# A lightweight convolution and a gated MLP on one core: one third of block 0's convolution as two TensorE steps over four shifted copies of x

## The chip, the cores and the metric

The kernel runs on one core of one Trainium2 chip. A time is the device time of one execution in microseconds (us). Three executions of the kernel before took 2196.03, 2195.52 and 2195.48 us; the median is 2195.52. A profile is one further execution, recorded by the hardware; its span runs from its first to its last instruction.

The engines are named as in the profile: PE is the matrix engine (TensorE), PEld its weight loads, DVE the vector engine, ACT the scalar engine, POOL GpSimd, SP the engine that here only issues DMAs. L231 means line 231 of the kernel before.

## The reference

Only the shapes and formulas that matter are kept.

```python
# x: (8, 4096, 192) f32; weight: (8 heads, 7 taps) f32
w = softmax(weight, axis=-1)
y[b, s, c] = sum_k w[head(c), k] * x_pad[b, s + k, c]     # 6 zeros ahead of each sequence
# y as (32768, 192); w_in: (192, 2048); w_out: (2048, 192), both scaled by a float64 number
h = y @ w_in
g = h * clip(h + 3.0, 0.0, 6.0) / 6.0
out = (g @ w_out).astype(float32)
```

Each head owns 24 channels. The two weight matrices arrive as 64-bit floating-point numbers; x and the taps are 32-bit.

## The kernel before

**Tiling.** The 32768 tokens are cut into 32 blocks of 1024, each in two halves of 512. x is laid out with channels first. A channel is 3p + s, with p from 0 to 63 and s from 0 to 2: partitions 0 to 63 of a tile hold the 64 values of p for the first half of the tokens, partitions 64 to 127 the same for the second half, and s, called a third, is an axis of the free dimension. Six columns ahead of the tokens hold the tokens before (zeros at the head of a sequence).

**First layer.** The hidden units are 16 chunks of 128. Every f32 product is made of three passes in a reduced format: high part of the weight by high part of y, low part by high part, full weight by low part of y (`PASSES`). So y of each third is split into high (`high_of`, ACT) and low (`low_of`, DVE: y minus high). A unit n of the first layer is one chunk, for both halves of the tokens: `products` issues, per third, six matmuls, two per pass, one on each half of the partitions. Units 0 to 7 take y as it is (`y_own`); units NP to NP + 7 (NP is 8) take `y_other`, in which the two halves of the partitions are swapped by two DMAs per part and third (`swap`, SP, L304 and L305). With the results in PSUM, ACT makes `relu` (L316) and DVE `gate` (L320) writes the hidden value into g.

**Second layer.** It multiplies g by w_out; in block 0 directly (`direct_chunk`, L331), in later blocks by a recursive scheme with fewer products.

**Rounding of the weights.** A unit of 384 weights per partition comes in by DMA as 64-bit words and becomes f32 in four steps of class `Rounding`: `split` (two integer operations on DVE, L192 and L196), `clamp` (three on ACT, L204, L207, L210), `join` (two on DVE, L213 and L217, then a product on POOL, L221), and for w_in `part`: the high part on ACT (L229), a full copy (L230) and the low part, full minus high (L231), both on POOL. The units are, in order, w_in 0, w_in 1, w_in 2, w_out 0, w_in 3, w_out 1 and so on.

**Block 0.** Its start is written out by hand; each engine runs its instructions in the order of the source (`manual_schedule`, from L909). Third 2 is convolved on PE: seven matmuls with a diagonal matrix per tap (`pe_tap`, L924) into PSUM bank b, after three matmuls of zeros (L932). Third 0 is convolved on DVE, seven taps of two cuts each (`conv_units`, L289 and L293). Third 1 is shared: tap 0 on ACT (L938), tap 1 on DVE, taps 2 to 6 on PE in bank b1, and a DVE addition (L983) puts the parts together. The order around this is:

```python
high_y(pe_third, psum[:, b : b + 1])     # ACT, then two swaps on SP
part(0)                                  # ACT L229, POOL L230 and L231
for u in conv0[per - 3 : per]:           # the last three DVE operations of third 0
    u()
low_y(pe_third, psum[:, b : b + 1])      # DVE L428, then two swaps
high_y(0, all_of(0))                     # ACT L425, then two swaps
low_y(0, all_of(0))
thirds_of(0, pe_third, 0)                # unit 0: thirds 2 and 0
thirds_of(NP, pe_third)                  # unit NP: third 2, from y_other
```

After that come unit w_in 1 (split, clamp, join, part), the end of third 1, the loads for later, `thirds_of(0, 1, end=True)` and `thirds_of(NP, 0)`. A loop over 16 steps (from L1026) then runs units in the order 0, 1, NP, NP + 1, 2, NP + 2 and so on. Each step issues the products of its unit (none for unit 0, the last third for unit NP), the relu, the steps of the weight units that are due, the gate, and from step 5 on every second step 16 products of the second layer.

**Queues.** SP issues, in this order, part of x, w_in 0, third 1 of x (two DMAs), w_in 1, w_in 2, w_out 0, w_in 3; then the swaps as their data come; then further weights and x of block 1. POOL issues third 2 of x, ACT the upper half of third 0.

Of the kernel before, what the change touches and what calls it, by code (L numbers as in the profile page):

```python
# [11 lines left out]
F32 = mybir.dt.float32  # L12
# [19 lines left out]
def kernel(  # L32
# [20 lines left out]
    K3 = D // D2  # L53
# [7 lines left out]
    NP = NC // 2  # L61
    DH = D // 2
    QS = 32
# [30 lines left out]
    for base, dma in ((0, nc.scalar), (D2, nc.sync)):  # L94
        dma.dma_start(
            out=w_sb[base : base + D2],
            in_=weight.unsqueeze(1).to_broadcast([H, GJ, KC]),
# [6 lines left out]
    def load_x0(s, dma_lower, dma_upper):  # L104
        head, lower, upper = x_source(0)
        dma_lower.dma_start(out=x_tiles[0][0:D2, s, head:], in_=lower[:, s])
        dma_upper.dma_start(out=x_tiles[0][D2:P, s, :], in_=upper[:, s])
# [6 lines left out]
    make_identity(nc, ident[:])  # L114
    diag = cnv.tile([P, KC, P], F32, name="diag", bufs=1)
    g = cst.tile([P, NP, 2, G, N], F32, name="g")
    mx = ot.tile([P, 1], F32, name="mx")
    zeros = g[:, 0, 0, 0]
    nc.vector.memset(zeros, 0.0)
# [31 lines left out]
    def load_w_in(j):  # L151
        st = early_stages[j]
        for half in range(2):
            nc.sync.dma_start(
                out=st[half * D2 : (half + 1) * D2].rearrange("p (s f) w -> p s (f w)", s=K3),
                in_=w_in_bits[j + half * NP].rearrange("p s f w -> p s (f w)"),
            )
        return st
# [14 lines left out]
    class Rounding:  # L173
# [4 lines left out]

        def __init__(self, load, dst):
            self.load_words, self.dst = load, dst

        def load(self):
            self.st = self.load_words()
# [1 line left out]
        def split(self, engine=nc.vector):  # L187
            high = self.st[:, :, 1]
            self.top = cnv.tile([P, WS], U32, name="top")
            self.scale = cnv.tile([P, WS], U32, name="scale")  # L190
            self.sig = cnv.tile([P, WS], F32, name="sig")
            engine.tensor_scalar(  # L192
                out=self.scale[:], in0=high, scalar1=0x7FF00000, scalar2=None,
                op0=ALU.bitwise_and,
            )
            engine.tensor_scalar(  # L196
                out=self.top[:], in0=high, scalar1=0xFFFFF, scalar2=0x100000,
                op0=ALU.bitwise_and, op1=ALU.bitwise_or,
            )
# [12 lines left out]
        def join(self):  # L212
            nc.vector.scalar_tensor_tensor(  # L213
                out=self.scale[:], in0=self.st[:, :, 1], scalar=0x80000000,
                in1=self.scale[:], op0=ALU.bitwise_and, op1=ALU.bitwise_or,
            )
            nc.vector.scalar_tensor_tensor(  # L217
                out=self.sig[:], in0=self.top[:], scalar=2.0**-20, in1=self.sig[:],
                op0=ALU.mult, op1=ALU.add,
            )  # L220
            nc.gpsimd.tensor_tensor(  # L221
                out=self.sig[:] if len(self.dst) > 1 else self.dst[0],
                in0=self.sig[:], in1=self.scale[:].bitcast(F32), op=ALU.mult,
            )

        def part(self):
            if len(self.dst) > 1:
                high, low, full = self.dst
                nc.scalar.mul(r32(high), self.sig[:], CUT)  # L229
                nc.gpsimd.tensor_copy(out=r32(full), in_=self.sig[:])  # L230
                nc.gpsimd.tensor_tensor(  # L231
                    out=r32(low), in0=self.sig[:], in1=high, op=ALU.subtract
                )

    def r32(ap):
        return ap.bitcast(F32R)

    def w_in_unit(j):
        dst = [w[:, j].rearrange("p s f -> p (s f)") for w in w_in_parts]
        return Rounding(lambda: load_w_in(j), dst)  # L240

    def w_out_unit(j):
        dst = w_out[:, j, B11 : B22 + 1].rearrange("p b d -> p (b d)")
# [14 lines left out]
    for n in range(5):  # L258
        units[n].load()
        if n == 0:  # L260
            load_x0(1, nc.sync, nc.sync)

    nc.vector.tensor_reduce(out=mx[:], in_=w_sb[:], axis=AX.X, op=ALU.max)
    e_sb = cst.tile([P, KC], F32, name="e_sb")
# [1 line left out]
        out=e_sb[:], in0=w_sb[:], in1=mx[:].to_broadcast([P, KC]), op=ALU.subtract  # L266
# [3 lines left out]
    c_sb = cst.tile([P, KC], F32, name="c_sb")  # L270
# [5 lines left out]
    y = ys.tile([P, K3, N], F32, name="y")  # L276
    OWN, OTHER = range(2)

    def conv_units(i, parts, cuts=1):


        x = x_tiles.pop(i)
        W = N // cuts

        def tap(part, k, t):
            c = c_sb[:, k : k + 1]
            to = y[:, part, t : t + W]
            if k == 0:
                nc.vector.tensor_scalar(  # L289
                    out=to, in0=x[:, part, t : t + W], scalar1=c, scalar2=None, op0=ALU.mult  # L290
                )
            else:
                nc.vector.scalar_tensor_tensor(  # L293
                    out=to, in0=x[:, part, k + t : k + t + W], scalar=c, in1=to,
                    op0=ALU.mult, op1=ALU.add,
                )

        return [
            lambda part=part, k=k, t=t: tap(part, k, t)
            for part in parts for k in range(KC) for t in range(0, N, W)  # L300
        ]

    def swap(to, part):
        nc.sync.dma_start(out=to[D2:P], in_=part[0:D2])  # L304
        nc.sync.dma_start(out=to[0:D2], in_=part[D2:P])  # L305
# [6 lines left out]
    psum = ps.tile([P, 2 * 4, N], F32, name="psum")  # L312
# [96 lines left out]
    def add(out, x, y, op=ALU.add):  # L409
        nc.vector.tensor_tensor(out=out, in0=x, in1=y, op=op)  # L410
# [13 lines left out]
    def high_of(out, x):  # L424
        nc.scalar.mul(r32(out), x, CUT)  # L425

    def low_of(out, x, high, engine):
        engine.tensor_tensor(out=r32(out), in0=x, in1=high, op=ALU.subtract)  # L428
# [480 lines left out]
    with tc.manual_schedule():  # L909
# [4 lines left out]
            out=c_sb[:], in0=e_sb[:], in1=sm[:].to_broadcast([P, KC]), op=ALU.mult  # L914
# [2 lines left out]

        thirds = [slice(s, s + 1) for s in range(K3)]
        pe_third = K3 - 1
        pe_taps = 2  # L920
        x0 = x_tiles[0]

        def pe_tap(b, part, k, first):
            nc.tensor.matmul(  # L924
                out=psum[:, b], lhsT=diag[:, k], rhs=x0[:, part, k : k + N],
                start=(k == first), stop=(k == KC - 1),
            )

        b, b1 = (2 * free_slots[-1] + k for k in range(2))
        for _ in range(3):  # L930

            nc.tensor.matmul(  # L932
                out=psum[:, b], lhsT=zeros[:, 0:P], rhs=zeros, start=True, stop=True
            )
        for k in range(KC):
            nc.scalar.mul(diag[:, k], ident[:], c_sb[:, k : k + 1])
            pe_tap(b, pe_third, k, 0)
        nc.scalar.mul(y[:, 1], x0[:, 1, 0:N], c_sb[:, 0:1])  # L938
        for k in range(pe_taps, KC):
            pe_tap(b1, 1, k, pe_taps)  # L940

        early = {}

        def thirds_of(n, *which, end=False):
            if n not in early:
                early[n] = free_slots.pop(0)
            for s in which:
                products(n, early[n], s, begin=s == pe_third, end=end)

        def high_y(s, of):  # L950
            high_of(y_own[HIGH][:, thirds[s]], of)
            swap(y_other[0][:, HIGH, thirds[s]], y_own[HIGH][:, thirds[s]])

        def low_y(s, of):
            low_of(y_own[LOW][:, thirds[s]], of, y_own[HIGH][:, thirds[s]], nc.vector)
            swap(y_other[0][:, LOW, thirds[s]], y_own[LOW][:, thirds[s]])

        def all_of(s):
            return y[:, thirds[s]]

        conv0 = conv_units(0, thirds[:pe_third], 2)
        per = len(conv0) // pe_third
        for u in conv0[:5]:
            u()
        split(0)
        clamp(0)
        for u in conv0[5 : per - 3]:
            u()
        join(0)
        high_y(pe_third, psum[:, b : b + 1])  # L970
        part(0)
        for u in conv0[per - 3 : per]:
            u()
        low_y(pe_third, psum[:, b : b + 1])
        high_y(0, all_of(0))
        low_y(0, all_of(0))
        thirds_of(0, pe_third, 0)
        thirds_of(NP, pe_third)
        split(1)
        clamp(1)  # L980
        for u in conv0[per + 2 : per + 2 * pe_taps]:
            u()
        add(y[:, 1], psum[:, b1], y[:, 1])  # L983
        high_y(1, all_of(1))
        join(1)
        part(1)
        low_y(1, all_of(1))
        for n in (5, 6, 7, 8):
            load(n)
        x_tiles[1] = load_x(1)  # L990
        split(2)
        clamp(2)
        thirds_of(0, 1, end=True)
        thirds_of(NP, 0)

        def conv_jobs(i, add_last=False):

# [28 lines left out]
        for r in range(2 * NP):  # L1026
            k = order[r]
# [11 lines left out]
            n = joins.get(r)  # L1039
# [128 lines left out]
```

## Time and profile before

| What | Value |
|---|---|
| Median of three executions | 2195.52 us |
| The profiled execution's own time | 2195.4 us |
| Its span | 2193.6 us |
| Granted PE clock over the span | 0.999 |
| First matmul of the first layer (L443) | starts at 17.18 us |
| First relu (L316) | starts at 22.63 us |
| Second relu | starts at 23.83 us |

The page gives, for each engine, the busy time, its share of the span and the number of instructions; the chain that ended last, followed back from the last instruction through what released each step; groups of instructions with the mean duration; and the DMA issues. The timeline gives for each row the start, the duration over all instructions of the row, the engine, the line, the operation, output and inputs, the shape, and how many; in brackets stands the idle time before it and what ended that. A row with the engine's name and a q behind it is the queue that issues, so SPq is SP issuing a DMA. Matmuls of f32 appear twice per call, as two instructions.

### The profile page before, as it was taken

What the parts mean: (1) busy time and instruction counts of PE and PEld (TensorE: products, weight loads), DVE (VectorE), ACT (ScalarE), POOL (GpSimd) and SP (SyncE); (2) the same over time, 40 slices, a digit from 0 to 9 for tenths busy, and PEclk for the clock granted to TensorE, in tenths of its full rate; (3) what the DMA queues carried; (4) which work ended last, traced back from release to release, by engine and by line L of the source; (5) the groups of instructions that cost most, each with busy time, mean ns of one, the idle gap of its engine ahead of it and who ended that gap; (6) DMA issues with size and microseconds to landing.
All of it is one profiled execution on the core that took longest, in us unless ns stands there. A gap on an engine that the chain in (4) does not pass through costs nothing.

```text
span 2193.6 us, 53710 instructions
## 1 busy us (share of the span) xinstructions
PE 2185.0 (100%) x23086; PEld 1564.3 (71%) x23086; DVE 1979.9 (90%) x1871; ACT 1271.8 (58%) x1761; POOL 1018.1 (46%) x867
## 2 busy tenths in 40 slices
PE   9999999999999999999999999999999999999998
PEld 5577777777777777777777777777777777777776
DVE  8889899889899898998989988999999999898987
ACT  7456565565655665555656556565566555565644
POOL 4545543355433555334554335553355543455433
PEclk9999999999999999999999999999999999999999
DMA  7366556756567665666655675656666566765564
GB/s 166 66 120 98 97 99 111 128 90 107 97 111 121 103 109 91 110 112 120 98 97 100 112 127 90 107 98 112 121 106 106 91 110 112 122 97 97 99 105 64
DMA packets 329821, 231.80 MB, mean 106 GB/s; under 512 B 208816, under 2 KB 293296, under 8 KB 329584
## 3 DMA queue, kind: packets, MB, share of 16 engines
q0 software_dynamic: 98752, 122.35, 36.6%
q1 hardware_dynamic: 229320, 105.73, 23.8%
q8 instruction: 181, 2.97, 0.6%
q10 hardware_dynamic: 1512, 0.30, 0.1%
q14 instruction: 56, 0.46, 0.1%
HBM read 31.72 MB, written 25.17 MB: 26 GB/s over the span
## 4 chain that ended last, share of the span: by engine, by line
PE 98%; ACT 1%; DVE 0%; POOL 0%; DMA 0%; issue 0%; POOLq 0%; DVEq 0%
PE psum L583 49%; PE psum L443 47%; PE psum L331 2%; PE psum L924 0%; PE psum L932 0%; ACT g L316 0%; DVE results L410 0%; DMA y_other<-y 0%; POOL w_in L231 0%; ACT scale L207 0%; POOL out_dram L357 0%; ACT sig L204 0%; ACT sig L210 0%; POOL sig L221 0%; DVE xt L833 0%
## 5 line engine op out<-in xcount | busy, mean ns | idle before, releaser
L583 PE MATMUL psum<-g,w_out 128*32 128x512 f32 (+1 forms) x5720 | 1023.8, 508 | 0.0
L316 ACT ACTIVATE g<-psum,half 128x1024 f32<-128x1024 f32 x512 | 571.5, 1116 | 312.4 <-PE psum L443 311.2
L583 PE MATMUL psum<-s,w_out 128*32 128x512 f32 (+1 forms) x3272 | 735.5, 570 | 0.9 <-DVE results L410 0.9
L320 DVE SCALAR_TENSOR_TENSOR g<-g,psum 128x1024 f32<-128x1024 f32 x512 | 609.4, 1212 | 133.1 <-ACT g L316 132.8
L541 POOL TENSOR_TENSOR s<-g 128x256 f32<-128x256 f32 x248 | 254.3, 1025 | 751.3 <-DMA out_dram<-results 538.5
L583 PEld LDWEIGHTS psum<-g,w_out 128*32 128x32 f32 x5720 | 421.4, 110 | 171.1 <-issue 61.6
L443 PE MATMUL psum<-y,w_in 64*128 64x512 f32 x4608 | 534.3, 388 | 0.3
L443 PE MATMUL psum<-y_other,w_in 64*128 64x512 f32 x4608 | 529.0, 386 | 0.0
L443 PEld LDWEIGHTS psum<-y,w_in 64*128 64x128 f32 x4608 | 428.6, 184 | 120.7 <-issue 26.0
L443 PEld LDWEIGHTS psum<-y_other,w_in 64*128 64x128 f32 x4608 | 431.6, 184 | 91.0 <-DMA y_other<-y 0.4
L1007 DVE SCALAR_TENSOR_TENSOR y<-x,c_sb,y 128x1536 f32<-128x1536 f32 x156 | 306.1, 1962 | 1.9 <-ACT y L1004 1.8
L583 PEld LDWEIGHTS psum<-s,w_out 128*32 128x32 f32 x3272 | 227.9, 110 | 106.6 <-issue 54.3
L583 PE MATMUL psum<-g,w_s 128*32 128x256 f32 x1488 | 289.3, 379 | 0.0
L390 POOL TENSOR_TENSOR s<-g 128x1024 f32<-128x1024 f32 x93 | 236.9, 2717 | 0.4 <-DVE g L320 0.4
L583 PE MATMUL psum<-z,w_s 128*32 128x256 f32 x992 | 235.1, 380 | 0.0
L390 DVE TENSOR_TENSOR s<-g 128x1024 f32<-128x1024 f32 x124 | 188.9, 1543 | 1.1
L583 PEld LDWEIGHTS psum<-g,w_s 128*32 128x32 f32 x1488 | 149.8, 110 | 32.0
L583 PE MATMUL psum<-s,w_s 128*32 128x256 f32 x744 | 170.7, 379 | 0.0
L483 ACT ACTIVATE z<-g 128x512 f32<-128x512 f32 x186 | 142.6, 767 | 18.5 <-DVE g L320 18.5
L410 DVE TENSOR_TENSOR g<-g 128x1024 f32<-128x1024 f32 x124 | 143.6, 1220 | 1.1
L410 DVE TENSOR_TENSOR results<-psum,results 32x256 f32<-32x256 f32 (+2 forms) x221 | 107.9, 488 | 39.1 <-PE psum L583 33.8
L541 POOL TENSOR_TENSOR s<-s,g 128x256 f32<-128x256 f32 x124 | 136.4, 1100 | 9.7
(115 smaller groups left out, 2347.8 us busy)
## 6 DMA issues: line engine op xcount, KB each, us to landing
y_other<-y SPq DMA_DIRECT2D x124, 384.0 KB, 5.1
z<-g POOLq DMA_DIRECT2D x93, 512.0 KB, 5.6
z<-z POOLq DMA_DIRECT2D x62, 512.0 KB, 5.4
out_dram<-results SPq DMA_DIRECT2D x375, 64.0 KB, 2.6
y<-x POOLq DMA_DIRECT2D x30, 768.0 KB, 8.9
x<-in_x_dram SPq DMA_DIRECT2D x53, 388.5 KB, 7.4
g<-g POOLq DMA_DIRECT2D x31, 512.0 KB, 6.4
g<-in_moe_w_in_dram SPq DMA_DIRECT2D x16, 192.0 KB, 5.5
```

The source lines that it names most:

```text
L316: nc.scalar.activation(r6, h, ACT.Relu, bias=half[:], scale=1.0 / 6.0)
L320: nc.vector.scalar_tensor_tensor(out=g_, in0=g_, scalar=1.0, in1=h, op0=ALU.min, op1=ALU.mult)
L331: lambda p=p: nc.tensor.matmul(out=bank[j * QS : (j + 1) * QS, tokens], lhsT=w_out[:, p, w, cols], rhs=x[:, p, tokens], start=(first and p ...
L390: engine.tensor_tensor(out=o[:, r], in0=a[:, r], in1=b[:, r], op=op)
L410: nc.vector.tensor_tensor(out=out, in0=x, in1=y, op=op)
L443: nc.tensor.matmul(out=psum[:, 2 * slot + k], lhsT=r32(w_in_parts[wn][r, c, s]), rhs=r32(y_other[0][r, yn, s] if group else y_own[yn][r, s ...
L483: nc.scalar.mul(to, x, sign)
L541: engine.tensor_tensor(out=o, in0=p, in1=q, op=op)
L583: nc.tensor.matmul(out=out, lhsT=w, rhs=x, start=start, stop=True, tile_position=(0, j * QS), skip_group_check=True,)
L1007: nc.vector.scalar_tensor_tensor(out=y[:], in0=taps_of(k), scalar=c_sb[:, k : k + 1], in1=y[:], op0=ALU.mult, op1=ALU.add,)
```

## The change

Third 1 of block 0's convolution is no longer shared by three engines. Four copies of its x are loaded (`x_quads`), each on 32 partitions and each shifted by one more token; both token halves stand in one row of 1028 columns, and the 64 values of p are split into two groups a of 32. A matrix of 128 by 32 (`quad_diag`) holds four taps' diagonals, one below the other, so that one matmul does four taps of 32 channels; step j = 0 does taps 0 to 3, step j = 1 taps 4 to 6. The eight matmuls (two steps, two halves, two groups) write the four 32-partition strips of bank b1. The copies into `quad_diag` are eight small ACT operations. The memory of `x_quads` is the part of g of chunks 2 and 3, which is not in use yet.

Tap 0 on ACT, tap 1 on DVE, five taps on PE and the addition for third 1 go; its high and low parts are taken from bank b1.

Unit w_in 0 becomes urgent: its product and its low part move from POOL to DVE and its full copy from POOL to ACT. The other units stay.

The order changes too: after join(0) come high_y(2), part(0) and then five DVE operations of third 0 (three before, with two fewer ahead of join(0)); split(1) moves ahead of high_y(0); third 0 of unit NP moves ahead of third 1 of unit 0; low_y(1) moves ahead of part(1).

```diff
+    QW = TB + 4
+    x_quads = (
+        g[:, 2:4].rearrange("p c h k n -> p (c h k n)")[:, : 2 * QW]
+        .rearrange("p (a u) -> p a u", a=2)
+    )
+    nc.vector.memset(x_quads[:, :, 0:PAD], 0.0)
+    quad_diag = cnv.tile([P, 2, 2, QS], F32, name="quad_diag", bufs=1)
+    nc.gpsimd.memset(quad_diag[3 * QS :, :, 1], 0.0)
+
+    def load_x_quads(s, dma):
+        rows_ = xT[0].rearrange("(a p s) t -> s p a t", a=2, s=K3)[s]
+        for r in range(4):
+            dma.dma_start(
+                out=x_quads[r * QS : (r + 1) * QS, :, PAD - r :],
+                in_=rows_[..., 0 : QW - PAD + r],
+            )
...
-            nc.gpsimd.tensor_tensor(
+            (nc.vector if self.urgent else nc.gpsimd).tensor_tensor(
                 out=self.sig[:] if len(self.dst) > 1 else self.dst[0],
...
-                nc.gpsimd.tensor_copy(out=r32(full), in_=self.sig[:])
-                nc.gpsimd.tensor_tensor(
+                if self.urgent:
+                    nc.scalar.copy(out=r32(full), in_=self.sig[:])
+                else:
+                    nc.gpsimd.tensor_copy(out=r32(full), in_=self.sig[:])
+                (nc.vector if self.urgent else nc.gpsimd).tensor_tensor(
                     out=r32(low), in0=self.sig[:], in1=high, op=ALU.subtract
...
-            load_x0(1, nc.sync, nc.sync)
+            load_x_quads(1, nc.sync)
...
+        def quad_weights():
+            for r in range(4):
+                for a in range(2):
+                    ch = slice(a * QS, (a + 1) * QS)
+                    ks = range(r, KC, 4)
+                    nc.scalar.copy(
+                        out=quad_diag[r * QS : (r + 1) * QS, a, 0 : len(ks)],
+                        in_=diag[ch, r::4, ch],
+                    )
+
+        def pe_quads(b):
+            for j in range(2):
+                for h in range(2):
+                    for a in range(2):
+                        q = 2 * h + a
+                        nc.tensor.matmul(
+                            out=psum[q * QS : (q + 1) * QS, b], lhsT=quad_diag[:, a, j],
+                            rhs=x_quads[:, a, h * N + 4 * j : (h + 1) * N + 4 * j],
+                            start=j == 0, stop=j == 1,
+                            tile_position=(0, q * QS), skip_group_check=True,
+                        )
...
-        nc.scalar.mul(y[:, 1], x0[:, 1, 0:N], c_sb[:, 0:1])
-        for k in range(pe_taps, KC):
-            pe_tap(b1, 1, k, pe_taps)
...
-        conv0 = conv_units(0, thirds[:pe_third], 2)
-        per = len(conv0) // pe_third
+        conv0 = conv_units(0, thirds[:1], 2)
         for u in conv0[:5]:
             u()
         split(0)
         clamp(0)
-        for u in conv0[5 : per - 3]:
+        quad_weights()
+        pe_quads(b1)
+        for u in conv0[5:9]:
             u()
         join(0)
         high_y(pe_third, psum[:, b : b + 1])
         part(0)
-        for u in conv0[per - 3 : per]:
+        for u in conv0[9:]:
             u()
         low_y(pe_third, psum[:, b : b + 1])
+        split(1)
         high_y(0, all_of(0))
         low_y(0, all_of(0))
         thirds_of(0, pe_third, 0)
-        thirds_of(NP, pe_third)
-        split(1)
+        thirds_of(NP, pe_third, 0)
         clamp(1)
-        for u in conv0[per + 2 : per + 2 * pe_taps]:
-            u()
-        add(y[:, 1], psum[:, b1], y[:, 1])
-        high_y(1, all_of(1))
+        high_y(1, psum[:, b1 : b1 + 1])
         join(1)
+        low_y(1, psum[:, b1 : b1 + 1])
         part(1)
-        low_y(1, all_of(1))
...
         thirds_of(0, 1, end=True)
-        thirds_of(NP, 0)
```

More of the change, by code (lines that the diff above doesn't have):

```diff
@@ L173, with __init__ @@
     class Rounding:
-        def __init__(self, load, dst):
-            self.load_words, self.dst = load, dst
+        def __init__(self, load, dst, urgent=False):
+            self.load_words, self.dst, self.urgent = load, dst, urgent
         def load(self):
@@ L236, in r32 @@
         return ap.bitcast(F32R)
+    URGENT = 1
     def w_in_unit(j):
         dst = [w[:, j].rearrange("p s f -> p (s f)") for w in w_in_parts]
-        return Rounding(lambda: load_w_in(j), dst)
+        return Rounding(lambda: load_w_in(j), dst, j < URGENT)
     def w_out_unit(j):
@@ L919, with pe_tap @@
         pe_third = K3 - 1
-        pe_taps = 2
         x0 = x_tiles[0]
-        def pe_tap(b, part, k, first):
+        def pe_tap(b, part, k):
             nc.tensor.matmul(
                 out=psum[:, b], lhsT=diag[:, k], rhs=x0[:, part, k : k + N],
-                start=(k == first), stop=(k == KC - 1),
+                start=(k == 0), stop=(k == KC - 1),
             )
+        def quad_weights():
[18 more added lines that the diff above has]
+                        )
         b, b1 = (2 * free_slots[-1] + k for k in range(2))
@@ L936 @@
             nc.scalar.mul(diag[:, k], ident[:], c_sb[:, k : k + 1])
-            pe_tap(b, pe_third, k, 0)
-        nc.scalar.mul(y[:, 1], x0[:, 1, 0:N], c_sb[:, 0:1])
-        for k in range(pe_taps, KC):
-            pe_tap(b1, 1, k, pe_taps)
+            pe_tap(b, pe_third, k)
         early = {}
```

## The prediction

> **What bounds the kernel now.** I read the page's busy rows first, then the chain that ended last in order of time over the first 60 us, then each engine's timeline there.
>
> ```profile
> PE 2185.0 (100%) x23086; PEld 1564.3 (71%) x23086; DVE 1979.9 (90%) x1871; ACT 1271.8 (58%) x1761; POOL 1018.1 (46%) x867
> ```
> ```profile
> PE 98%; ACT 1%; DVE 0%; POOL 0%; DMA 0%; issue 0%; POOLq 0%; DVEq 0%
> ```
>
> TensorE (PE) is the bound of the whole; what is not PE on the chain lies in the start. A start that is x us shorter or longer moves the end by about x, as everything behind it is one PE stream. The edit touches only the first 25 us. The chain there (start, us, what):
>
> ```profile
> 6.95 6.02 PE psum L924 x14
> ...
> 13.00 0.60 ACT y L425
> ...
> 22.14 1.67 PE psum L443 x12
> ...
> 23.83 1.12 ACT g L316
> ...
> 35.26 3.71 PE psum L443 x30
> ```
>
> The reader is to see the hand-over at 23.83. From that second relu (unit 1, L316) ACT runs without a gap to 34.1, through relus, clamps and the high part of w_in 3 at 33.59; POOL's subtraction at 34.18 follows, and at 35.26 PE has its operands and never starves again. That 11.4 us relay is untouched by the diff. So the price of the edit is the shift of this relu, which waits for the last matmul of products(1). What sets that today is on the weight-load queue (PEld) and SP:
>
> ```profile
> 18.28 0.59 SPq L305 DMA_DIRECT2D y_other<-y  x1
> ```
> ```profile
> 20.64 0.19 PEld L443 LDWEIGHTS psum<-y_other,w_in 64*128 64x128 f32 x2 [0.40 <-DMA y_other<-y]
> ...
> 22.14 1.22 PEld L443 LDWEIGHTS psum<-y,w_in 64*128 64x128 f32 x12 [0.57 <-POOL w_in L231]
> ```
>
> The swap of low(third 0) is issued at 18.28 and its landing lets PE on at 20.64: 2.35 us. PE then waits for w_in 1's low part at 22.14, runs twelve loads, and the relu starts 0.47 after the last (23.36 to 23.83). SP issues one pair of swaps every 1.28 us (starts at 16.42, 17.70, 18.98, 20.27), whatever its data do.
>
> DVE and ACT in the stretch that is rewritten:
>
> ```profile
> 8.84 2.46 DVE L293 SCALAR_TENSOR_TENSOR y<-x,c_sb,y 128x256 f32<-128x256 f32 x6
> 11.21 0.55 DVE L213 SCALAR_TENSOR_TENSOR scale<-g,scale 128x384 uint32<-128x384 uint32 x1
> 11.73 0.56 DVE L217 SCALAR_TENSOR_TENSOR sig<-top,sig 128x384 f32<-128x384 uint32 x1
> 12.21 2.26 DVE L293 SCALAR_TENSOR_TENSOR y<-x,c_sb,y 128x256 f32<-128x256 f32 x3
> 14.50 0.69 DVE L428 TENSOR_TENSOR y<-psum,y 128x512 fp32r<-128x512 f32 x1
> ```
> ```profile
> 13.00 0.60 ACT L425 ACTIVATE y<-psum 128x512 fp32r<-128x512 f32 x1 [1.29 <-PE psum L924]
> 13.58 0.52 ACT L229 ACTIVATE w_in<-sig 128x384 fp32r<-128x384 f32 x1
> ```
>
> Taps cost 0.41 each while POOL is idle and 0.75 beside POOL's three operations of unit 0 (12.38 to 15.33). ACT reaches the high part of w_in 0 (L229) only after high_y(2), which waits for PE's taps until 13.00.
>
> **The change part by part.**
>
> PE, third 1: five taps go, ten matmuls at a pitch of 0.43 (24 from 6.77 to 17.25), 4.3 us. In come eight 32-column matmuls, sixteen instructions. Nearest row: L331, 128*32 128x512, 32 in 3.64 us, four side by side; sixteen are 1.75. PE would finish at 12.97 + 1.75 = 14.7 instead of 17.25, plus at most the 0.35 and 0.84 that PEld idles on entering L331 and returning to L443. This gain is worth nothing unless PE then has operands.
>
> ACT: tap 0 of third 1 goes (L938, 0.72, which waited for x to 9.24), so clamp(0) starts at about 8.68, when the first split operation is done, and ends at 10.53. Eight small copies for quad_weights follow: between the 0.21 of the 128x7 exponential and the 0.29 pitch of the seven 128x128 diagonals (2.15 us for seven); I take 0.25, nearer the small end: 2.0, over at 12.5 (bounds 12.2 and 12.9). Hidden, since high_y(2) waits for PE to 13.0 anyway. The full copy of w_in 0 comes to ACT: 0.52, to 14.6, before anything else there is ready.
>
> SP and DMA: two loads of x (0.26 MB) become four of 0.26 MB: 0.79 MB and two issues (1.2 us) more, ahead of w_in 1, 2, 3 and w_out 0 on SP. At the 245 GB/s that the slices show at 8 to 9 us that is 3.2 us: the last copy lands at about 9.1 + 3.3 = 12.4 (today's x lands for 9.24), w_in 1 at about 14.3, the queue runs dry near 17.6 instead of 14.3. Cover: PE has nothing to do after the quads until 17.3 (below), and split(1) is reached at 17.3. Priced at nothing; cover gone, each us late is a us.
>
> POOL loses unit 0's 1.17 + 0.58 + 1.15; the two memsets are 0.1 at most in the idle start.
>
> DVE: taps 1 and the add of third 1 go (0.87 + 0.69); unit 0's product and subtraction come (about 0.55 each, as L213). But their place adds a wait. Taps 5 to 8 now end at 10.5, join(0) with its product at 12.0. The next DVE instruction is the subtraction high-from-full of unit 0, which needs ACT's L229: 13.58 + 0.52 = 14.1. DVE, in order, stands from 12.0 to 14.1 with five taps behind it that need nothing. Today POOL did this wait while DVE went on. Then: subtraction to 14.6; five taps at 0.41, to 16.7; low_y(2), 0.69, to 17.36 (today 15.19).
>
> From there everything that feeds PE is late:
> - Swaps: low(2) is issued at 17.39 (today 15.22), high(0) at 18.67, low(0) at 19.95 and, its second half, 20.53. It lands 2.35 later: 22.88 (today 20.63).
> - w_in 1: split(1) 17.3 to 17.9; clamp(1) on ACT 17.67 to 19.5; high_y(1) to 20.15; join(1) to 20.1; POOL's product to 21.2 (1.02; 21.5 at the 1.40 it took today), its low part by 22.85 to 23.2 (today 22.09).
> - PE: thirds_of(NP, 2, 0) now stands ahead of third 1 of unit 0. So when low(0) lands at 22.88, two loads of it, six of third 1 and eighteen of products(1) are still to run: 26 at 0.113 (18 in 2.04, L443) is 2.94, last load over at 25.8, relu at 25.8 + 0.47 = 26.3. The w_in 1 low part is asked for after fourteen of them, at 24.5: covered by 1.3.
>
> Sum: 26.3 against 23.83, **+2.5 us**. The relay behind it keeps its length, as its own ACT work and PE's work after products(1) are the same. On the profiled execution, 2195.4 (span 2193.6, 0.12 under the median 2195.52), that is **2197.9**. Bounds of the terms: copies (none), swap pitch 1.20 to 1.29 (-0.2), landing 2.3 to 2.4, join and taps (+-0.3), memset ahead of the warm-up matmuls (+0.1): 2197.0 to 2198.8 if the mechanism holds.
>
> The clock: the same 128x512 f32 matmul took 1.04 to 1.22 us for the first six (L932) and 0.59 from L924 on, so PE starts at about half pace, though the granted clock reads 1.00 in every slice. [...]
>
> **The rivals.**
>
> 1. No stall, no loss. If DVE could run the five taps before the subtraction (ACT through with L229 by 12.0, or another order on DVE than the source's), low(2) would be issued at 14.9 as the first pair ends, low(0)'s second half at 18.0, land at 20.4, and the relu start at 23.8: no change, 2195.4; with the pair pitch at 1.0 (the shortest issue is 0.46) 0.7 less, 2194.7. It decides if low(0)'s second half is issued before 18.07. Against: ACT idled 1.29 for PE before 13.00, and every DVE operation today stands in source order. The 0.4 us or more needed for a real gain isn't there even so: the swap queue takes over.
>
> [...]
>
> 3. The loads behind the copies come late. w_in 1 has 14.3 to 17.3 at DVE plus the 1.3 at PE in hand; at the 106 GB/s of the 14 to 15 us slice the 1.05 MB would take 9.9 us from 8.1, w_in 1 would land near 21.7, 4.4 after DVE wants it, and the end be 3 later still: 2201. Against: while loads alone run, no slice from 4 to 14 us is under 219.
>
> **How the numbers follow.** The stall case has 0.75, rival 1 0.12, rival 2 0.08, rival 3 0.05. Predicted 2197.9. The range reaches from just under rival 1's no-change end, 2195.2, to 2199.9: it leaves out rivals 2 and 3 and rival 1's lower half, 0.19. 0.2%, about what a measurement of this kernel can tell from no change, is 4.4 us: 2191.1 to 2199.9. No case gives 2191; 0.01 for what I haven't seen. Slower: most of rivals 2 and 3 and a tail of the first, 0.09. Within: 0.90.
>
> **What would show it.** Right: DVE idle about 2.1 us before the subtraction at 14.1, released by ACT's high part; low(2) issued near 17.4; PEld waiting for y_other until near 22.9; sixteen quad matmuls in about 1.75 us; the second L316 relu near 26.3 and PE unbroken from about 37.7. Wrong: taps on DVE between 12 and 14, quads held by x_quads past 16, split(1) waiting for its load, matmuls of 0.2 us pitch near 23, or a relay of another length than 11.4.

## The result, and the profile after

The changed kernel takes 2200.05 us (median; 2198.50 to 2200.64) where the kernel before takes 2195.74 beside it: +4.3 us, a ratio of 1.0019 with a 95% interval of 1.0012 to 1.0027. That is 0.15 above 2199.9, the upper end of the forecast's range around 2197.9. The profiled execution took 2199.41 us with a span of 2197.6, 4.0 more than before. New line numbers are 19 to 25 higher: L231 is now L253, L229 L248, L293 L318, L425 L450, L428 L453, L304 and L305 L329 and L330, L316 L341, L443 L468, L331 L356. New are L958, the copies into `quad_diag`, and L968, the quad matmuls.

TensorE is the bound as before. The row of busy times on the page of the kernel after:

```profile
PE 2185.2 (99%) x23092; PEld 1565.2 (71%) x23092; DVE 1974.9 (90%) x1871; ACT 1272.7 (58%) x1769; POOL 1014.0 (46%) x865
```

PE has the same 2185 us to do, so the loss is idle time and slower work in the start. The chain there, kernel after (start, us, what):

```profile
18.93 3.71 DMA y_other<-y
...
22.69 5.63 PE psum L468 x25
...
28.34 1.12 ACT g L341
...
38.66 1.03 POOL w_in L253
...
39.73 3.71 PE psum L468 x30
```

The second relu starts at 28.34 instead of 23.83, 4.5 later. From it to the unbroken PE stream at 39.73 it is 11.39 us, against 11.43 before: the relay has kept its length, as forecast, and everything happened before 28.34. In place of the short wait for w_in 1 the chain now has a DMA of 3.71 us, a swap, ahead of PE's products.

The forecast's own steps first. The timelines of DVE, then of ACT, kernel after:

```profile
13.87 0.56 DVE L253 TENSOR_TENSOR w_in<-sig,w_in 128x384 fp32r<-128x384 f32 x1 [1.73 <-ACT w_in L248]
14.34 2.06 DVE L318 SCALAR_TENSOR_TENSOR y<-x,c_sb,y 128x256 f32<-128x256 f32 x5
16.43 0.69 DVE L453 TENSOR_TENSOR y<-psum,y 128x512 fp32r<-128x512 f32 x1
```
```profile
10.55 1.97 ACT L958 COPY quad_diag<-diag 32x64 f32<-32x64 f32 x8
...
13.31 0.52 ACT L248 ACTIVATE w_in<-sig 128x384 fp32r<-128x384 f32 x1
```

DVE stands idle for 1.73 us until ACT's high part of w_in 0 is there; the five taps and low_y(2) come behind. So the wait that the forecast was built on is real. The timeline of SP's queue, kernel after:

```profile
17.15 0.46 SPq L329 DMA_DIRECT2D y_other<-y  x1
...
20.23 0.59 SPq L330 DMA_DIRECT2D y_other<-y  x1
```

The first half of low(2)'s swap is issued at 17.15 (forecast 17.39), the second half of low(0)'s at 20.23 (forecast 20.53). Up to the issue of the swaps the forecast holds within 0.3 us. What follows is the timeline of the weight loads, kernel after:

```profile
20.68 0.50 PEld L468 LDWEIGHTS psum<-y_other,w_in 64*128 64x128 f32 x4 [2.17 <-DMA y_other<-y]
...
22.69 0.50 PEld L468 LDWEIGHTS psum<-y_other,w_in 64*128 64x128 f32 x4 [0.72 <-DMA y_other<-y]
23.69 0.29 PEld L468 LDWEIGHTS psum<-y_other,w_in 64*128 64x128 f32 x2 [0.50 <-DMA y_other<-y]
23.85 4.01 PEld L468 LDWEIGHTS psum<-y,w_in 64*128 64x128 f32 x24
```

PE gets low(0) at 23.69, not 22.88: 0.8. And the last 26 loads take from 23.69 to 27.86, 4.17 us, not 2.94: 1.2. Together 2.0, the distance from the forecast 26.3 to 28.34. Two other views of the kernel after name the two causes. The tile view of `y_other` over the first 32 us gives the time from a swap's issue to its landing, first after, then before:

```profile
DMA to landing us min/median/max: 2.8/3.7/6.6
```
```profile
DMA to landing us min/median/max: 2.3/2.3/2.4
```

Each swap took 2.3 us before; now the first one used, high(2), needs 6.6, and the next ones land one pair per 1.0 us: high(2) near 20.6, low(2) 21.7, high(0) 22.6, low(0) 23.7. The windows of 1 us, kernel after (us; busy time and count of PE, PEld, DVE, ACT, POOL; granted PE clock; DMA share; GB/s):

```profile
18.00:19.00 1.00, 0.73 (x4) 0.19 (x2) 0.54 (x2) 0.94 (x3) 0.00 (x0) 1.00 1.13 225
...
20.00:21.00 1.00, 0.32 (x2) 0.32 (x4) 1.00 (x2) 0.02 (x1) 0.94 (x1) 0.50 1.07 262
...
25.00:26.00 1.00, 1.00 (x8) 0.70 (x8) 0.00 (x0) 0.19 (x1) 0.48 (x1) 0.50 0.75 261
...
27.00:28.00 1.00, 1.00 (x12) 0.82 (x10) 1.00 (x1) 0.00 (x0) 0.00 (x0) 1.00 0.91 204
```

The same view of the kernel before:

```profile
14.00:15.00 1.00, 1.00 (x4) 0.43 (x3) 0.97 (x2) 0.60 (x2) 1.00 (x2) 1.00 0.48 106
...
20.00:21.00 1.00, 1.00 (x8) 0.39 (x6) 1.00 (x2) 0.55 (x2) 0.94 (x2) 1.00 0.92 209
```

Before, the loads have ended in the slice from 14 us, where the share drops to 0.48. In the kernel after, the DMA engines stay full until past 20 us (share 1.0 or more in every slice from 4 us on but one, of 0.94), because 0.79 MB more stand ahead of the swaps. And the granted clock falls to 0.50 shortly before 20 (0.90 in the slice from 19, 0.50 in the six from 20), where it was 1.00 before, and comes back in the slice from 26 (0.69): at 25 PE starts 8 matmuls in a microsecond, at 27 twelve.

### The profile page after: what moved, and what is told of

It reads as the page before. It is cut to its first block, busy times and chain, and to the rows that moved or that the text cites. A ratio compares the mean times of both kernels' runs of the same rounds, so it can differ in the third digit from the quotient of the medians.

```text
span 2197.6 us, 53730 instructions
## 1 busy us (share of the span) xinstructions
PE 2185.2 (99%) x23092; PEld 1565.2 (71%) x23092; DVE 1974.9 (90%) x1871; ACT 1272.7 (58%) x1769; POOL 1014.0 (46%) x865
## 4 chain that ended last, share of the span: by engine, by line
PE 98%; ACT 1%; DVE 0%; POOL 0%; DMA 0%; issue 0%; POOLq 0%; SPq 0%; DVEq 0%
PE psum L608 49%; PE psum L468 48%; PE psum L356 2%; PE psum L948 0%; PE psum L978 0%; ACT g L341 0%; DMA y_other<-y 0%; DVE results L435 0%; ACT scale L226 0%; ACT sig L223 0%; DVE y L318 0%; POOL out_dram L382 0%; DVE xt L858 0%; ACT w_in L248 0%; POOL p L821 0%
## 5 line engine op out<-in xcount | busy, mean ns | idle before, releaser
L341 ACT ACTIVATE g<-psum,half 128x1024 f32<-128x1024 f32 x512 | 571.4, 1116 | 317.0 <-PE psum L468 316.8
L468 PE MATMUL psum<-y,w_in 64*128 64x512 f32 x4608 | 535.4, 389 | 1.5 <-DVE y L453 1.3
L468 PE MATMUL psum<-y_other,w_in 64*128 64x512 f32 x4608 | 530.6, 387 | 2.1 <-DMA y_other<-y 2.1
L468 PEld LDWEIGHTS psum<-y,w_in 64*128 64x128 f32 x4608 | 429.7, 184 | 122.5 <-issue 26.8
L468 PEld LDWEIGHTS psum<-y_other,w_in 64*128 64x128 f32 x4608 | 432.1, 184 | 94.3 <-DMA y_other<-y 3.9
```

Source lines behind the costliest of these rows:

```text
L341: nc.scalar.activation(r6, h, ACT.Relu, bias=half[:], scale=1.0 / 6.0)
L468: nc.tensor.matmul(out=psum[:, 2 * slot + k], lhsT=r32(w_in_parts[wn][r, c, s]), rhs=r32(y_other[0][r, yn, s] if group else y_own[yn][r, s ...
```

## The experiments

**The theories.** Theory A is the forecast's: the wait on DVE makes the swaps late. Theory B: the copies' bytes make them late, since the swaps land behind the loads that SP issued earlier. A third part can add to either: the halved clock. All edits are made on the changed kernel unless another is named. Times are medians, beside the kernel before, measured together with each (2195.5 to 2195.7).

The table has, for each run, when PE's weight loads got low(0) and when the second relu started, both in its profile, and the time against before. A halved clock is a granted clock of 0.50 in two or more of the slices of 1 us, a full one is 1.00 in every slice from 15 to 28 us.

| Run | Wait on DVE | Bytes ahead of the swaps | Clock in the profile | low(0) at PE, us | Second relu, us | Against before, us |
|---|---|---|---|---|---|---|
| Kernel before | no | as before | full | 20.64 | 23.83 | 0 |
| Changed kernel | yes | +0.79 MB | halved | 23.69 | 28.34 | +4.3 |
| e1_no_stall | no | +0.79 MB | halved | 23.79 | 28.87 | +4.1 |
| e2_loads_later | yes | loads moved behind | halved, early | 23.35 | 26.63 | +3.8 |
| e3_both | no | loads moved behind | halved | 20.89 | 25.53 | +1.8 |
| e4_warm | yes | +0.79 MB | full | 23.52 | 26.82 | +2.7 |
| e5_both_warm | no | loads moved behind | full | 21.16 | 24.43 | +1.7 |
| e6_order | no | loads moved behind | full | no wait for it | 24.28 | +1.7 |
| e7_before_copies | kernel before | +0.79 MB | full | 23.64 | 26.25 | +2.2 |
| e8_swaps_pool | no | +0.79 MB, later loads too | halved | 26.47 | 31.10 | +7.5 |
| e9_no_stall_warm | no | +0.79 MB | full | 23.64 | 26.95 | +4.0 (+2.6 in the group of the profile) |
| e10_one_copy | yes | as before | full | 22.36 | 25.65 | +2.5 |
| e11_one_copy_no_stall | no | as before | full | 20.65 | 23.96 | +0.5 |
| e12_pairs | no | +0.26 MB | full | 21.15 | 23.75 | -0.4 |

**e1_no_stall: the wait taken away.** The high and low part of w_in 0 come behind the five taps.

```diff
-        part(0)
         for u in conv0[9:]:
             u()
+        part(0)
```

> The five DVE taps of third 0 stand ahead of unit 0's subtraction, nothing else moves, so DVE no longer waits 1.73 us for ACT. Theory A, the forecast's: the wait makes the swaps late. Then low(2) is issued near 15.3 instead of 17.15, the second half of low(0) near 18.3 and lands 2.35 later, at 20.7; the second relu starts near 24.1 and the time is about 2196.0. Theory B: the swaps lie in SP's DMA queue behind 0.79 MB more of loads, the last of which (w_in 3) lands near 19.5, and land one pair per 1.0 us after that, whenever they are issued. Then low(0) still lands at 23.6 and PE is held as now: the second relu at 27 to 28.4, the time 2198.8 to 2200.0.

Measured: 2199.63 (2198.70 to 2200.63), ratio 1.0019 (1.0009 to 1.0029). Nothing is won. low(2) is issued at 15.69, 1.5 earlier than in the changed kernel, yet the timelines of the weight loads and of ACT in this run read:

```profile
20.73 0.44 PEld L468 LDWEIGHTS psum<-y_other,w_in 64*128 64x128 f32 x4 [3.70 <-DMA y_other<-y]
...
23.79 0.29 PEld L468 LDWEIGHTS psum<-y_other,w_in 64*128 64x128 f32 x2 [0.52 <-DMA y_other<-y]
```
```profile
28.87 1.12 ACT L341 ACTIVATE g<-psum,half 128x1024 f32<-128x1024 f32 x1 [1.85 <-PE psum L468]
```

The swaps land at the same times as with the wait, to 0.1 us: issued 1.5 us earlier, low(2) only takes longer to land here. Theory A falls as the only cause.

**e2_loads_later: the queue ahead of the swaps made shorter.** Two of the units that are loaded ahead of the swaps, w_out 0 and w_in 3, come behind them.

```diff
-    for n in range(5):
+    for n in range(3):
...
-        for n in (5, 6, 7, 8):
+        for n in (3, 4, 5, 6, 7, 8):
```

> The loads of w_out 0 and w_in 3 (0.79 MB, as much as the copies add) are issued after the last swap instead of ahead of the first; the DVE wait stays. Theory A: swaps are issued as now (low(2) at 17.15, low(0)'s second half at 20.2); they land 2.35 to 3.5 later; a gain of at most 1.2, if the clock stays halved 2198.8. Theory B: the queue is empty before 17, every swap lands 2.35 after its issue, high(2) near 16.4, so PE works on unit NP from 19 on; low(0) lands at 22.6, the second relu starts at 26.0 with a full clock: 2197.9, what the forecast had.

Measured: 2199.29 (2198.52 to 2200.41), ratio 1.0017 (1.0008 to 1.0026). The timelines of SP's queue and of the weight loads in this run:

```profile
20.98 0.60 SPq L330 DMA_DIRECT2D y_other<-y  x1
```
```profile
23.35 0.19 PEld L468 LDWEIGHTS psum<-y_other,w_in 64*128 64x128 f32 x2 [0.99 <-DMA y_other<-y]
```

PE has the swaps 2.3 to 2.4 us after the issue of their second halves again (18.41 to 20.75, 19.70 to 22.05, 20.98 to 23.35), so it is those loads that they had waited behind; but with the wait on DVE the second half of low(0) is issued at 20.98 and is at PE at 23.35. The clock is low in the slices from 18 to 21 (0.50, 0.50, 0.50 and 0.84), before PE has much to do, and at 1.00 for the 26 loads; the relu starts at 26.63. Then the units that were moved are late: PE waits 0.86, 0.90 and 1.88 between 31 and 39 us, and is unbroken from 40.35, 13.7 behind the relu. So this run shows the landing cured and the gain spent further on.

**e3_both: both edits.**

> No DVE wait and the two loads behind the swaps. Both theories: low(2) issued near 15.3, low(0) lands near 20.7, PE never idle long enough for its clock to be halved, the second relu near 24.1, the time 2196.0 (before 2195.7). Theory A expects the no-wait kernel alone to be as fast as this one; theory B expects that only this one gets there.

Measured: 2197.28 (2196.34 to 2197.78), ratio 1.0007 (0.9998 to 1.0017). Against before, the two together win 2.5 us on the changed kernel's +4.3, singly 0.2 and 0.5. low(0) is at PE at 20.89, 0.25 later than in the kernel before. The clock of the profiled execution is low all the same (0.68, 0.50, 0.50 and 0.61 in the four slices from 20), though PE's weight-load queue is never idle for more than 0.98 us there, and 24 loads take 3.99 us.

**e4_warm: the clock.** Three matmuls of zeros into a bank that is free then, one within the products of third 2 of unit 0 and two ahead of those of unit NP, so that PE has work while it waits.

```diff
-        thirds_of(0, pe_third, 0)
+        def warm(n):
+            for _ in range(n):
+                nc.tensor.matmul(
+                    out=psum[:, 4], lhsT=zeros[:, 0:P], rhs=zeros, start=True, stop=True
+                )
+
+        early[0] = free_slots.pop(0)
+        products(0, early[0], pe_third, (0, 1), begin=True)
+        warm(1)
+        products(0, early[0], pe_third, (2,))
+        thirds_of(0, 0)
+        warm(2)
```

> Three matmuls of zeros into a bank not in use yet (0.86 us each at full clock) fill PE's two idle stretches, one near 16 and two near 18.8; nothing else moves. Theory C: the halved clock of 19.8 to 26.6 costs the 26 matmuls up to the second relu 4.17 us instead of 2.94, and makes the times scatter. Then the granted clock reads 1.0 in every slice, the second relu starts near 27.1, and the time is 2198.8 with a scatter as before. If the landings alone set it, the time stays 2200.0.

Measured: 2198.17 (2197.86 to 2198.39), ratio 1.0012 (1.0003 to 1.0021). A window and the weight loads of this run:

```profile
20.00:21.00 1.00, 1.00 (x4) 0.30 (x4) 1.00 (x2) 0.00 (x0) 0.99 (x1) 1.00 1.07 270
```
```profile
23.52 0.19 PEld L468 LDWEIGHTS psum<-y_other,w_in 64*128 64x128 f32 x2 [0.68 <-DMA y_other<-y]
23.63 2.72 PEld L468 LDWEIGHTS psum<-y,w_in 64*128 64x128 f32 x24
```

The clock stays at 1.00, 24 loads take 2.72 instead of 4.01, and low(0) lands as late as before the edit. The halved clock is therefore worth about 4.3 - 2.7 = 1.6 us of the result. The times scatter over 0.5 us here and over 2.1 in the changed kernel; but e10 and e11, with the same zeros, scatter over 1.6 and 1.3, so it is not shown that the clock makes the scatter.

**e5_both_warm and e6_order: all three edits, then the old order of unit NP too.** e6 puts the last third of unit NP back behind third 1 of unit 0.

> No DVE wait, the two loads behind the swaps, and the three matmuls of zeros in PE's idle stretches. If the wait, the queue and the clock are all there is beside the new order of unit NP: low(0) lands near 20.9 as in the kernel without the zeros, the 26 loads behind it take 2.94 instead of 4.16, the second relu starts near 24.3, and the time is 2196.0, with a scatter of 0.6. If the halved clock is not what held that kernel up, 2197.3 again.

> The same, with third 0 of unit NP behind third 1 of unit 0, as before the change: 20 loads instead of 26 stand behind the landing of low(0). If the order costs what it was given, 6 x 0.113 = 0.7: the second relu near 23.6, the time 2195.3. If w_in 1's parts or low(1) then end last, no gain: 2196.0.

Measured: 2197.21 (2196.96 to 2197.98) and 2197.24 (2196.67 to 2197.97), ratios 1.0008 (0.9999 to 1.0017) and 1.0008 (0.9998 to 1.0017). The relus start at 24.43 and 24.28, 4 us earlier than in the changed kernel, but only 2.6 come out at the end (+1.7 against before). The timeline of DVE in e6_order shows where the rest stays:

```profile
26.81 0.36 DVE L211 TENSOR_SCALAR scale<-stage 128x384 uint32<-128x384 uint32 x1 [2.88 <-DMA stage<-in_moe_w_out_dram]
```

It is the load of w_out 0, moved behind the swaps. This re-ordering doesn't put the bytes out of the way: ahead of the swaps the loads delay these, behind them they are the next wait. The order of unit NP is worth nothing ahead of that wait; what it is worth without it, these two runs don't show.

**e7_before_copies: the bytes alone, on the kernel before.** The loop of `load_x_quads` runs over r from 1 to 3 here: three shifted copies are loaded behind third 1 of x, into the same unused part of g, and never read.

```diff
             load_x0(1, nc.sync, nc.sync)
+            load_x_quads(1, nc.sync)
```

> The kernel before with three of the four copies of x (0.79 MB) loaded right behind third 1 of x, and not used: the queue's part alone. Theory B: w_in 3 lands near 19 instead of 15.3, the swaps one pair per 1.0 us behind it, low(0) near 23.4 instead of 20.6; twenty loads behind it: the second relu near 26.2 at full clock, the time 2197.9, up to 2199.5 if PE's clock is halved meanwhile. Theory A: the loads lie beside other work, 2195.5 to 2196.

Measured: 2197.68 (2196.62 to 2198.80), ratio 1.0010 (1.0001 to 1.0019): +2.2 us, from bytes that nobody reads. The timelines of the weight loads and of ACT in this run:

```profile
23.64 0.19 PEld L458 LDWEIGHTS psum<-y_other,w_in 64*128 64x128 f32 x2 [0.74 <-DMA y_other<-y]
```
```profile
26.25 1.12 ACT L331 ACTIVATE g<-psum,half 128x1024 f32<-128x1024 f32 x1 [2.31 <-PE psum L458]
```

low(0) arrives at the moment it does in the changed kernel (23.69), and 3.0 later than in the kernel before. Here the granted clock stayed at 1.00 in every slice from 15 to 28, with PE idle from 18.3 to 20.6. That is one execution: seven of the ten took up to 2197.81, three from 2198.62, and one of these three shows the mean granted clock of the changed kernel, 0.998, which none of the seven does. Part of the upper end may be the clock's.

**e8_swaps_pool: another queue for the swaps.** On e1, POOL issues block 0's swaps instead of SP.

```diff
-            swap(y_other[0][:, HIGH, thirds[s]], y_own[HIGH][:, thirds[s]])
+            swap(y_other[0][:, HIGH, thirds[s]], y_own[HIGH][:, thirds[s]], (nc.gpsimd, nc.gpsimd))
```

`swap` takes the issuing queues as an argument here; the low part's swap is edited the same way.

> The changed kernel without the DVE wait (2199.6), with block 0's swaps issued by POOL, whose DMA queue is another one than SP's; the loads stay ahead on SP. If the swaps wait for their turn in SP's queue: they pass the loads, high(2) lands near 17, low(0) near 21, the second relu is at 24.4 to 25.6, the time 2196.5 to 2197.7. If the 16 engines' bytes alone set it, they land after 23 all the same: 2199.6.

Measured: 2203.00 (2202.03 to 2203.97), ratio 1.0034 (1.0021 to 1.0047). high(2), issued at 13.41 and 13.95, is used at 21.62; a later swap takes 8.38 us on the chain. The run is confounded: SP, which no longer waits for the swaps' data, sent the next weights and x of block 1 between 13.0 and 19.8. So it shows that the swaps from POOL did not get past the other transfers here, and not whether a queue of their own would help with SP's order unchanged.

**e9 to e11: the square.** e9 is e1 with the zeros of e4. e10 is e4 with one copy loaded instead of four; the quads read its 32 rows only, so that the bytes are as before and the wait is there. e11 is e10 with the edit of e1. In e10 and e11 only taps 0 and 4 of third 1 are computed; PE's instructions keep their number.

```diff
-        for r in range(4):
+        for r in range(1):
...
-                            out=psum[q * QS : (q + 1) * QS, b], lhsT=quad_diag[:, a, j],
-                            rhs=x_quads[:, a, h * N + 4 * j : (h + 1) * N + 4 * j],
+                            out=psum[q * QS : (q + 1) * QS, b], lhsT=quad_diag[0:QS, a, j],
+                            rhs=x_quads[0:QS, a, h * N + 4 * j : (h + 1) * N + 4 * j],
```

> The changed kernel without the DVE wait and with the matmuls of zeros: all copies loaded, full clock. Of a square of four (DVE wait or not, four copies or one, full clock in all) this is the corner of bytes without wait. If the queue of bytes holds the swaps whenever they are issued: low(0) lands near 23.5 as with the wait, the second relu near 26.8, the time 2198.1, as the kernel with wait and zeros (2198.2). If the wait were the larger cause: 2196.5.

> The changed kernel with the matmuls of zeros, of which only the first of the four copies of x is loaded (0.26 MB, as much as before the change) and the quad matmuls read its 32 rows alone, so six taps of third 1 are left out of the result; the number of matmuls stays. Wait without bytes. This is the case that the forecast priced: swaps land 2.35 after their issue, low(0) near 22.6, the second relu near 26.1, the time 2197.9. If the copies' bytes are the only cause: 2196.

> The same without the DVE wait: neither wait nor bytes, six taps of third 1 left out again. low(0) lands near 20.7, the second relu near 24.1, the time 2195.9: what is then left over the kernel before is the order of unit NP. If it stays near 2197.9, the wait isn't what makes the kernel with one copy slow.

Measured: e10 2198.06 (2197.26 to 2198.85), ratio 1.0011 (1.0002 to 1.0020); e11 2196.03 (2195.51 to 2196.80), ratio 1.0002 (0.9993 to 1.0011). The wait alone costs 2.0 us between these two, 2.5 against before. Their intervals overlap, but the slowest execution of e11 (2196.80) is below the fastest of e10 (2197.26). The weight loads of e10, then of e11, where low(0) is as early as in the kernel before:

```profile
22.36 0.19 PEld L468 LDWEIGHTS psum<-y_other,w_in 64*128 64x128 f32 x2 [0.93 <-DMA y_other<-y]
...
26.53 2.15 PEld L468 LDWEIGHTS psum<-y_other,w_in 64*128 64x128 f32 x20 [0.89 <-DMA y_other<-y]
```
```profile
20.65 0.19 PEld L468 LDWEIGHTS psum<-y_other,w_in 64*128 64x128 f32 x2 [0.52 <-DMA y_other<-y]
```

e9 came out at 2199.54 (2197.99 to 2200.22), ratio 1.0016 (1.0008 to 1.0025), in two groups: five executions up to 2198.63 and six from 2199.54. The profiled one, 2198.22, is of the lower: full clock, low(0) at 23.64, relu at 26.95. The groups stand about as far apart as the price of the clock, and in the profile the zeros end at 20.0 while the first swap comes at 20.62 (in e4 they last past it). The mean granted clock of each execution points the same way: 0.999 or 1.000 in the lower group, 0.998 in three of the upper six, as in the changed kernel. That the clock was halved in the upper group is therefore likely, but no profile shows it. So of the corner "bytes without the wait" the clean figure is +2.6, from one group, and e7's +2.2 stands beside it.

The square at full clock is then: neither +0.5, wait alone +2.5, bytes alone +2.2 to +2.6, both +2.7. Each alone costs nearly what both cost together: over the corner with neither, e11, it is 2.0, 2.1 (e9) and 2.2. They hold back the same event, the landing of low(0), and lie beside each other: the later of the two counts, not their sum. The landings in the profiles show it directly: 20.65 with neither, 22.36 with the wait, 23.64 with the bytes, 23.52 with both. That is why e1 won so little; in e2 the loads that were moved took back a part as well.

**e12_pairs: fewer bytes.** Two copies on 64 partitions each instead of four on 32, and four steps of 64-channel parts; 0.26 MB more than before instead of 0.79, and two copies on ACT instead of eight. No wait on DVE (e1's edit), and unit NP in the old order.

```diff
-        for r in range(4):
+        for r in range(2):
...
-            for j in range(2):
+            for j in range(4):
...
-                            start=j == 0, stop=j == 1,
-                            tile_position=(0, q * QS), skip_group_check=True,
+                        start=j == 0, stop=j == 3,
+                        tile_position=(0, h * D2), skip_group_check=True,
```

> Two copies on 64 partitions each and four steps instead of four copies and two steps: 0.26 MB more than before the change instead of 0.79, eight 64-column matmuls of 2 x 4 x 0.43 = 3.4 us on PE instead of 1.75; no DVE wait, the order of unit NP as before the change. The loads end about 1.1 us later than before the change, low(0) lands near 20.8, twenty loads behind it: second relu at 23.2 to 23.6, time 2195.0 to 2195.4. If even 0.26 MB delays the swaps: 2196 or more.

Measured: 2195.19 (2194.60 to 2195.46), ratio 0.9997 (0.9989 to 1.0006): 0.4 us under the kernel before, against 4.3 over it for the changed kernel. The 0.4 is a difference that the interval doesn't tell from none. The timelines of PE and of ACT in this run:

```profile
12.40 3.65 PE L960 MATMUL psum<-g,pair_diag 128*64 128x512 f32 x16
```
```profile
23.75 1.12 ACT L338 ACTIVATE g<-psum,half 128x1024 f32<-128x1024 f32 x1 [1.26 <-PE psum L465]
```

The taps take 3.65 us on PE instead of 1.92, and this costs nothing: after the products that follow, PE still waits 0.94 us on its weight-load queue, until 18.16, for the first swap; low(0) is at PE at 21.15, the relu starts where it does before. What the edit saved on PE was never on the path. Bytes, wait and order were changed together here, so this run doesn't say how much each of them gave.

## Why the prediction was wrong

- **The wait on DVE** came as forecast: 1.73 us idle (forecast 2.1) released by ACT, five taps in 2.06 (2.05), low(2) issued at 17.15 (17.39). Rival 1, no stall, is out.
- **The price of that wait** came out right, in part by luck. With the bytes as before and the clock full (e10) it is +2.5, 2198.06 against the forecast 2197.9. But the path is another: the relu starts at 25.65, not 26.3, and PE next waits 0.89 for a swap of third 1, until 26.53, which the sum didn't have; and 0.5 of the 2.5 is there without the wait too (e11).
- **The eight copies on ACT** took 1.97 (forecast 2.0), hidden. **The quads** took 1.92 (1.75) and started 0.4 later than forecast, without effect.
- **The step that failed first**, in order of time, is the one on SP and DMA, "Priced at nothing". Its cover was named for the quads and for w_in 1, and both were in fact in time. But the same queue carries the swaps, and these, the operands that PE waited for, were costed at their old 2.35 us. The queue ran dry near 19.5 rather than 17.6: 3.54 MB from 2.9 to 19.5 us are 213 GB/s, not 245. Even at the forecast 17.6 the swaps of high(2), issued at 13.31, had loads ahead of them. The term measures +2.2 to +2.6 alone (e7, e9), but lying beside the wait it adds only about 0.2 to it (e4 against e10), which the 1.6 us of scatter in e10 don't tell from none: low(0) lands 1.2 later, but in e10 PE has its next wait, for third 1's swap, which in e4 is covered.
- **The second step that failed**, and the larger in size, is the 26 loads at 0.113. They took 4.17 instead of 2.94, with the granted clock at 0.50 in the six slices from 20, and the clock as a whole is worth about 1.6 us (e4) of the 1.8 by which the result exceeds the forecast's +2.5. A start with all 26 loads at half pace is the forecast's rival 2, 2200.2 at a chance of 0.08: an estimate from 1.06 us for the first matmuls of the kernel before (L932) against 0.59 for the later ones, 1.8 times 0.113 for each load, +2.3. That PE goes to half pace as it waits was the author's assumption; no run of the kernel before shows it, but the changed kernel does. It cost the loads 1.2 and not 2.3, since the clock came back in the slice from 26 (0.69), before the last of them. The waits of the kernel before, 0.40, 0.21 and 0.57 us on the weight-load queue between 20.2 and 22.1, at 1.00 in every slice, were three of 1.18 us in all; those that came from 18.5 on were four, of 0.50 to 2.17 and 3.89 in all, and the first told nothing of the second. Whether the clock would have fallen at that time with the wait alone, no run shows, since e10 has the zeros; in e2, with the wait and the loads moved, it fell earlier (0.95 in the slice from 17, 0.50 in the next) and was at 1.00 again for the 26 loads.
- **Rival 3** looked at the right queue but at the wrong transfer: w_in 1 came in time, the swaps didn't.
- **The relay** of 11.4 held. The relu's shift of 4.5 became 4.0 at the end of the profiled span; where the 0.5 came back was not traced.

Summed in this order: +2.5 for the wait as forecast, about +0.2 for the bytes beside it, +1.6 for the clock: +4.3. With the bytes first, they would have most of the 2.7 and the wait next to nothing.

## What to carry to other kernels

When bytes are added ahead of a queue, price every later transfer on it, the small on-chip ones above all, and not only the loads next in line: 0.79 MB made a 2.3 us swap take up to 6.6. Two delays of the same event hide each other, so that undoing either shows little (0.2 us in e1; 0.5 in e2, which also made later loads late) and only a run without both, or each added alone to the kernel before, gives their price. A saving on an engine that waits for operands was worth nothing here: the pairs, 1.7 us slower on PE but with a third of the added bytes, without the wait on DVE and in the old order of unit NP, end 4.7 us ahead of the quads.

## What the runs showed of the hardware that was not expected

The granted clock of TensorE fell to 0.50, in the six slices from 20, with no PE gap over 1.87 us (changed kernel), and in two slices, those from 21 and 22, in e3_both with four gaps of at most 0.98 us on the weight-load queue, while in the profile of e7_before_copies 2.2 us of idle PE time did not lower it (1.00 in every slice from 15 to 28). PE was busy for 0.73, 0.73 and 0.00 us in the slices at 17, 18 and 19, late in the last of which it fell, in the changed kernel; for 0.77 and 0.57 in those at 18 and 19, before it fell in the next, in e3_both; and for 0.34, 0.00 and 0.43 in those at 18, 19 and 20 in e7_before_copies, where it didn't fall. So in these three profiles neither the longest gap nor PE's work in the slices just before tells whether the clock falls; what does, no run here shows. Three matmuls of zeros, into a bank that nobody reads, kept the clock up in every execution of e4_warm, as far as the mean granted clock (0.999 or 1.000 in all ten) and the times (within 0.5 us of each other) tell, but not, it seems, in every one of e9.
